# Attention and highway layer in one kernel: query turns in quarters of the array, one shared turning place, a new list of steps

## The chip, the cores and the metric

The kernel runs on one core of one Trainium2 chip. The metric is the device time of one execution in microseconds (us), lower is better. Five engines work side by side, each through its own instructions in order: TensorE (PE, matrix products and turns), VectorE (DVE), ScalarE (ACT), GpSimd (POOL) and SyncE (SP, which here only issues DMA transfers). TensorE writes to PSUM, eight banks of 2 KiB for each of the 128 partitions. Semaphores make one engine wait for another.

## The reference

Linear attention over 8 batches of 8 heads, 576 rows and 64 columns a head, then a highway layer over the 4608 rows of 512 columns that the heads give together:

```python
q_s = softmax(q, axis=-1)                    # over the 64 columns of a head
k_s = softmax(k, axis=2)                     # over the 576 rows
kv  = einsum('bhsd,bhse->bhde', k_s, v)
x   = einsum('bhsd,bhde->bhse', q_s, kv)     # -> rows b*s, columns h*d
H   = maximum(x @ w_h, 0)
T   = 1 / (1 + exp(-(x @ w_t + b_t)))
out = T * H + (1 - T) * x
```

All inputs and the output are float32; 30.4 MB are read and 9.4 MB written.

## The kernel before, in words

The rows are worked in 36 tiles of 128. A batch gives four tiles, and each pair of batches a ninth that takes the last 64 rows' worth of both (tiles 0 to 3 batch 0, 4 to 7 batch 1, 8 both, 9 to 12 batch 2, and so on; lines 125 to 129). Tiles 0, 4 and 5 are worked in two halves.

For a batch b the steps are, by their names in the list:

- `k`, `q`, `v`, `w`, `b`: transfers in, all on SP but the bias.
- `eq`, `ek` (ACT): exponentials of the queries and keys to float16; `vc` (POOL, some on ACT or DVE): v to float16.
- `kv` (PE): for each pair of heads 64x64 products of 65 columns (the 65th sums the keys), 72 a batch, on the four quarters of the array in turn (L269). `kr`, `kn` (DVE): the quotient, written into a block form for two heads at once.
- `qt` (PE): turns of the exponentials of the queries, so that the head's columns lie on the partitions; three groups a batch, of 8, 8 and 2 turns of 128x128 (L319, L324). They go into PSUM tile `qps`, which has a bank of its own. `qc` (DVE or ACT, L333) copies them to `eq` in SBUF. Two groups of batch 7 are turned by DMA instead (`qd`).

For a tile i:

- `xu` (PE, L361): turned queries times kv, with the sums in a 65th column; `rs`, `x` (DVE, L370 and L376): the quotient, to x in float16.
- `xt` (PE, L384): four turns of x into PSUM tile `turned`; `xe` (DVE or ACT, L391) copies them to `xT`.
- `bw`: the bias into the bank `tps`, as an ACT copy of a broadcast bias (L399) or as a PE product with ones (L401). `mt` (PE, L411): four products of x with w_t on top. `mh` (PE, L419): four products with w_h / 2 (less the identity, `whd` and `whc` at the start), into `gps`.
- `th` (ACT): tanh of half of it; `dd` (DVE, L439): the relu part; `uu`: (1 + tanh) times that, in one DVE instruction (L453) or in two on POOL (L450, L451; `:P` in the list); `oo` (POOL, L471): plus x; `st`: the store.

The order is written out by hand: `ORDER` (lines 16 to 62) is a list of 683 steps, each with the engine after a colon where there is a choice, and the kernel emits them in that order under a manual schedule. Each engine's instructions stand in the list's order, and a step waits for the steps ahead of it in the list that touch what it touches. `fill` steps are products of zeros into `turned` that keep PE at work at the start. PSUM: `tps` two banks, `gps` two, `xu` and kv two together, `qps` one, `turned` one.

The start of the list runs: loads of batch 0, w_h, w_t, then batch 1 (`k_1_2 v_1_2 q_1_0 k_1_0 v_1_0 q_1_4`). The loads of k, q and v have three buffers each, so that a load waits for the batch three back.

Of the kernel before, what the change touches and what calls it, by code (L numbers as in the profile page):

```python
# [8 lines left out]
FP32 = mybir.dt.float32  # L9
# [12 lines left out]
wtc_2:P whc_2:A mh_1_0 wtc_0:P vc_1_3 ek_1_3 ek_1_2 vc_1_0 xe_3_0:D mh_3_0 dd_1 xt_0_1 xt_0_0 mt_1_0 xe_0_0:D mh_0_0
xe_0_1 dd_3 xt_2_0 mh_0_1 mt_0_1 th_1_0 xe_2_0:D dd_0 vc_1_2:A kv_1_1 uu_1_0 oo_1_0 eq_1_0 mt_0_0 th_0_0 ek_1_0 ek_1_1
kr_1_1 bw_3 qt_1_0 vc_1_1:A kn_1_1 qc_1_0 mt_3_0 xu_5_1 uu_0_0 mh_2_0 th_3_0 bw_2 rs_5_1 x_5_1 dd_2 xu_4_1 kv_1_0
kr_1_0 eq_1_1 rs_4_1 xt_5_1 mt_2_0 th_2_0 kn_1_0 bw_5 xe_5_1:D x_4_1 xu_5_0 mt_5_1 qt_1_1 eq_1_2 rs_5_0 x_5_0 xt_5_0
xu_4_0 bw_4:A uu_3_0:P oo_3_0 xe_5_0:D mh_5_1 rs_4_0 x_4_0 mh_5_0 xt_4_1 qc_1_1:A xt_4_0 xe_4_1:D dd_5 eq_2_0 xe_4_0:D
v_4_0 mt_5_0 th_5_0 xu_6_0 qt_1_2 rs_6_0 qc_1_2 oo_0_0 mt_4_1 mh_4_1 mh_4_0 uu_2_0:P x_6_0 mt_4_0 eq_2_1 xt_6_0 xu_8_0
uu_5_0 bw_6:A xe_6_0:D qt_2_0 rs_8_0 x_8_0 mh_6_0 oo_5_0 th_4_0 xt_8_0 dd_4 uu_4_0 xu_7_0 mt_6_0 ek_2_0:F rs_7_0
vc_2_2:A bw_8 xe_8_0:D mt_8_0 x_7_0 th_6_0 xt_7_0 th_8_0 oo_2_0 vc_2_0 kv_2_0 oo_4_0 qc_2_0 q_4_0 bw_7:A qt_2_1
qc_2_1:A dd_6 uu_6_0:P oo_6_0 eq_3_0:F xe_7_0:D kr_2_0 kn_2_0 mh_8_0 xu_9_0 rs_9_0 x_9_0 mt_7_0 th_7_0 bw_9 dd_8  # L30
uu_8_0:P qt_2_2 qc_2_2:A xu_10_0 bw_10:A xt_9_0 xe_9_0:D rs_10_0 x_10_0 ek_3_0 mh_7_0 dd_7 ek_3_2 mh_9_0 xu_12_0 k_4_0
xt_10_0 k_5_0 rs_12_0 qt_3_0 xe_10_0:D x_12_0 mt_9_0 th_9_0 uu_7_0:P q_4_9 dd_9 xu_11_0 qc_3_0 vc_3_2:A xt_12_0
mt_10_0 rs_11_0 mh_10_0 x_11_0 v_5_0 q_5_0 vc_3_0 st_1_1 q_5_9 uu_9_0 dd_10 oo_7_0 kv_3_0 qt_3_1 th_10_0 oo_8_0 st_1_0
xe_12_0 bw_12:A mh_12_0 kr_3_0 qc_3_1:A kn_3_0 xu_14_0 rs_14_0 x_14_0 bw_11:A xt_11_0 xe_11_0 mt_12_0 th_12_0 qt_3_2
v_6_0 xt_14_0 oo_9_0 k_6_0 xu_13_0 q_6_0 xe_14_0 mh_11_0 dd_12 qc_3_2 mt_11_0 rs_13_0 eq_4_0:F th_11_0 uu_12_0
uu_10_0:P x_13_0 dd_11 xu_15_0 rs_15_0 vc_4_0 mh_14_0 x_15_0 st_5_1 dd_14 qt_4_0 oo_10_0 vc_4_2 xu_16_0 rs_16_0 x_16_0
# [24 lines left out]
st_35_1:A
"""


@with_exitstack
def kernel(
    ctx: ExitStack,
    tc: tile.TileContext,
    q: bass.AP,
    k: bass.AP,  # L70
    v: bass.AP,
# [5 lines left out]
    nc = tc.nc  # L77
# [456 lines left out]
```

## Time and profile before

| what | value |
|---|---|
| median of 3 runs | 119.03 us (119.0 to 119.74) |
| span of the profiled execution, first to last instruction | 116.9 us |
| lies around the span, against the median | 2.1 us |
| instructions | 3424 |
| HBM read, written | 30.41 MB, 9.44 MB |
| granted TensorE clock, mean | 0.995 |

The profiled execution's own time outside its span isn't in the profile; the median stands for it. In rows of groups the columns are line, engine, operation, output and inputs with shapes, count, then busy us and mean ns of one, then idle us ahead of them and what ended it. In the timeline and in the chain the first two numbers are the start and the length in us. A length of a PE row holds the pipeline's latency: the next step starts before that length is over. Busy times by stretch have busy us and counts of PE, PEld (weight load), DVE, ACT and POOL, then granted clock, DMA share and GB/s.

### The profile page before, as it was taken

The numbers are of one execution on the slowest core, as the hardware profiler recorded it, in microseconds if no ns is written. First come the engines' busy times: TensorE is split into PE (matmuls) and PEld (weight loads), VectorE is DVE, ScalarE is ACT, GpSimd is POOL, SyncE is SP. The second block draws the span as 40 slices with busy tenths as digits, with TensorE's granted clock in tenths as the row PEclk, the third lists the DMA queues.
The fourth block names the chain that finished last, engine by engine and source line by source line (L and its number), as shares of the span: only waits on it lengthen the run. The fifth ranks groups of instructions, "written<-read, shape, count | busy, mean of one in ns | idle before, by whom it ended". The sixth has DMA issues, their size and how long they took to land.

```text
span 116.9 us, 3424 instructions
## 1 busy us (share of the span) xinstructions
PE 109.5 (94%) x1351; PEld 61.6 (53%) x1351; DVE 93.3 (80%) x222; ACT 90.0 (77%) x132; POOL 89.1 (76%) x99
## 2 busy tenths in 40 slices
PE   5999987999999999999999999999999999999930
PEld 2354544545665656565665547566564555554520
DVE  5642587589799979979889798988989887899870
ACT  4356461897999999989999999998597998545520
POOL 5022237208996999999999999999989699999960
PEclk9999999999999999999999999999999999999998
DMA  2999999999999999999999999999999956992875
GB/s 42 399 392 377 408 398 385 375 377 379 393 391 397 383 391 393 358 375 387 357 376 360 387 392 363 390 381 383 399 398 217 302 204 270 397 404 115 315 295 179
DMA packets 24195, 40.58 MB, mean 347 GB/s; under 512 B 5362, under 2 KB 11762, under 8 KB 24180
## 3 DMA queue, kind: packets, MB, share of 16 engines
q1 hardware_dynamic: 24032, 40.24, 96.9%
q8 instruction: 10, 0.16, 0.6%
q10 hardware_dynamic: 148, 0.14, 0.4%
q14 instruction: 5, 0.04, 0.1%
HBM read 30.41 MB, written 9.44 MB: 341 GB/s over the span
## 4 chain that ended last, share of the span: by engine, by line
PE 67%; POOL 15%; issue 6%; DVE 5%; DMA 3%; SPq 1%; POOLq 0%; DVEq 0%
PE tps L411 18%; PE gps L419 16%; PE turned L167 9%; POOL o L471 7%; PE xu L361 6%; PE turned L384 5%; PE kv L269 5%; PE qps L324 4%; POOL u L451 4%; DMA out_dram<-o 3%; POOL g L450 2%; PE qps L319 2%; POOL v L259 2%; DVE x L376 2%; PE tps L401 1%
## 5 line engine op out<-in xcount | busy, mean ns | idle before, releaser
L471 POOL TENSOR_TENSOR o<-u,x 128x512 f32<-128x512 f16 (+1 forms) x36 | 40.6, 1143 | 1.6 <-DVE u L453 0.7
L411 PE MATMUL tps<-w16t,xT 128*128 128x512 f16 (+1 forms) x148 | 37.3, 373 | 0.0
L419 PE MATMUL gps<-w16h,xT 128*128 128x512 f16 x144 | 36.8, 379 | 0.5 <-DVE xT L391 0.5
L376 DVE TENSOR_TENSOR x<-xu,rs 128x512 f16<-128x512 f32 (+1 forms) x39 | 25.2, 649 | 2.4
L259 POOL CAST v<-v 128x1152 f16<-128x1152 f32 (+1 forms) x14 | 14.0, 1010 | 14.7 <-DMA v<-in_v_dram 13.7
L439 DVE SCALAR_TENSOR_TENSOR d<-x,gps 128x512 f16<-128x512 f16 x36 | 24.5, 680 | 0.3
L451 POOL TENSOR_TENSOR u<-g,d 128x512 f16<-128x512 f16 x17 | 19.7, 1158 | 1.7 <-DVE rs L370 0.4
L253 ACT ACTIVATE ek<-k 128x576 f16<-128x576 f32 (+2 forms) x15 | 17.9, 1225 | 3.0 <-DMA k<-in_k_dram 3.0
L419 PEld LDWEIGHTS <-xT 128*128 128x128 f16 x144 | 13.0, 98 | 12.3 <-DVE xT L391 1.8
L399 ACT COPY tps<-ball 128x512 f32<-128x512 f32 x28 | 16.6, 597 | 3.5 <-DVE u L453 3.2
L411 PEld LDWEIGHTS <-xT 128*128 128x128 f16 x148 | 13.2, 98 | 10.6 <-DVE xT L391 0.4
L361 PE MATMUL xu<-kvb,eq 128*128 128x130 f16 (+1 forms) x160 | 14.8, 224 | 0.2 <-DVE kvb L287 0.2
L384 PE MATMUL turned<-idh,x 128*128 128x128 f16 x144 | 14.2, 220 | 0.5 <-DVE x L376 0.5
L391 DVE COPY xT<-turned 128x512 f16<-128x512 f16 (+1 forms) x28 | 10.9, 391 | 4.2 <-PE turned L384 3.0
L435 ACT ACTIVATE tps<-tps 128x512 f32<-128x512 f32 (+1 forms) x20 | 11.2, 559 | 3.6 <-PE tps L411 3.3
L453 DVE SCALAR_TENSOR_TENSOR u<-tps,d 128x512 f16<-128x512 f32 (+1 forms) x19 | 12.7, 671 | 1.4 <-ACT tps L435 0.6
L361 PEld LDWEIGHTS <-eq 128*128 128x128 f16 (+1 forms) x160 | 10.0, 100 | 7.3 <-DVE x L376 2.5
L167 PE MATMUL turned<-blank 128*128 128x512 f16 x40 | 12.4, 458 | 1.5 <-POOL blank L149 1.3
L384 PEld LDWEIGHTS <-x 128*128 128x128 f16 x144 | 9.8, 98 | 6.0 <-DVE x L376 2.1
L307 ACT ACTIVATE qe<-q 128x1024 f16<-128x1024 f32 (+3 forms) x9 | 9.4, 1052 | 4.1 <-DMA q<-in_q_dram 4.1
L450 POOL TENSOR_SCALAR g<-th 128x512 f16<-128x512 f16 x17 | 10.6, 621 | 0.9 <-ACT th L433 0.9
L433 ACT ACTIVATE th<-tps 128x512 f16<-128x512 f32 x17 | 10.0, 594 | 0.9 <-PE tps L411 0.9
(48 smaller groups left out, 106.8 us busy)
## 6 DMA issues: line engine op xcount, KB each, us to landing
k<-in_k_dram SPq DMA_DIRECT2D x6, 1152.0 KB, 12.2
v<-in_v_dram SPq DMA_DIRECT2D x6, 1152.0 KB, 12.0
out_dram<-o SPq DMA_DIRECT2D x23, 256.0 KB, 4.0
q<-in_q_dram SPq DMA_DIRECT2D x10, 512.0 KB, 11.5
out_dram<-o SPq DMA_DIRECT2D x6, 512.0 KB, 3.8
k<-in_k_dram SPq DMA_DIRECT2D x4, 576.0 KB, 9.3
q<-in_q_dram SPq DMA_DIRECT2D x2, 1152.0 KB, 14.2
q<-in_q_dram SPq DMA_DIRECT2D x2, 640.0 KB, 10.5
```

What stands on the lines that cost most here:

```text
L167: nc.tensor.matmul(spare, blank[:, 0:P], blank, start=True, stop=True, skip_group_check=True)
L253: nc.scalar.activation(t[:, :, c:c + n].rearrange("p j c d -> p c j d"), T[f"k32{b}"][:, c:c + n].rearrange("p c (j d) -> p c j d", j=NJ), ...
L259: copy(v16[b % NV][:, c:c + n, :, 0:D], T[f"v32{b}"][:, c:c + n].rearrange("p c (j d) -> p c j d", j=NJ))
L361: nc.tensor.matmul(dst, turned_q(b, jp, n), kvb[b % NKV][:, hh, kk], start=True, stop=True, skip_group_check=True)
L376: nc.vector.tensor_mul(t[:, k0:k1], sums(i, k)[:, :, :, 0:64], T[f"rs{i}_{k}"][:, 0:k1 - k0].unsqueeze(3).to_broadcast([P, k1 - k0, 4, D]))
L384: nc.tensor.matmul(t[:, n], T[f"x{i}"][:, n0 + n % 2:n0 + 2 * P:2], idh, is_transpose=True, start=True, stop=True, skip_group_check=True)
L399: nc.scalar.copy(t[:, cs], ball[:, cs])
L411: nc.tensor.matmul(T[gate(i, k)][:, cs], T[f"xT{i}"][:, n], w16["t"][:, n, cs], start=False, stop=(n == parts[-1] and not first), skip_gro ...
L419: nc.tensor.matmul(t, T[f"xT{i}"][:, n], w16["h"][:, n], start=(first and n == parts[0]), stop=(n == parts[-1] and not (first and len(part ...
L439: nc.vector.scalar_tensor_tensor(t, T[f"x{i}"], -0.5, T[f"gps{i}"], op0=ALU.mult, op1=ALU.max)
L451: nc.gpsimd.tensor_mul(t, g, T[f"d{i}"])
L471: eng.tensor_add(t[:, cs], T[f"u{i}_{h}"][:, cs], T[f"x{i}"][:, cs])
```

## The change

- `qps` and its bank are gone. `turned` is now one PSUM tile of two banks, for turns of queries and of x alike. Query turns of the old kind lie in bank 0; x turns lie in bank 1, even tiles in its first half, odd tiles in its second.
- Query turns of batches 2 to 6, groups 0 and 1 (ten groups), are done by 32 turns of 64x64 on the four quarters of the array, the two halves of the rows into the two banks, so that such a group takes half of both banks. `qc` reads it from there in one instruction.
- `bw` can be a DVE copy (`:D`): 11 are, 19 are on ACT (28 before) and 7 on PE (9 before).
- The list is new (680 steps): w_t is loaded ahead of w_h, and batch 1 comes as `k_1_2 v_1_2 q_1_0 q_1_4 k_1_0 v_1_0`; 26 fill products where there were 40; 21 tiles have `uu` on POOL (17 before); 21 `xe` steps on DVE and 18 on ACT (28 and 11); 12 casts of v on POOL and 7 on ACT, five of these of the large kind (14 and 5, two large); one cast of w_t on ACT.

```diff
-    ps_q = pool("ps_q", 1, space=PS)
-    ps_xt = pool("ps_xt", 1, space=PS)
+    ps_ab = pool("ps_ab", 1, space=PS)
...
-    turned = ps_xt.tile([P, 2, 4, P], FP16, tag="xtps", name="turned")
-    spare = turned.rearrange("p a c d -> p (a c d)").bitcast(FP32)
+    turned = ps_ab.tile([P, 2, 2 * DM], FP16, tag="ab", name="turned")
+    spare = turned[:, 1].bitcast(FP32)
...
+    QUADS = (2, 3, 4, 5, 6)
+
+    def corners(b, g):
+        return b in QUADS and g < 2
+
+    def qt_corners(b, g):
+        t = turned[:, :, g * DM:(g + 1) * DM]
+        for n in range(8):
+            for r in range(2):
+                rows = slice(64 * r, 64 * r + 64)
+                for c in range(2):
+                    cols = slice(64 * c, 64 * c + 64)
+                    if b in WIDE:
...
+                        src = main[rows, 2 * g + n // 4, n % 2, n % 4 // 2, cols]
+                        dst = t[cols, r, 64 * n:64 * n + 64]
+                    else:
+                        j, kk = n // 2, n % 2
+                        src = T[f"qe{b}"][rows, 4 * g + j, 2 * kk + c]
+                        dst = t[cols, r].rearrange("p (a k t s u) -> p a k s t u", a=2, k=2, s=2, u=2)[:, j % 2, kk, j // 2]
+                    nc.tensor.matmul(dst, src, idh[rows, rows], is_transpose=True, start=True, stop=True,
+                                     skip_group_check=True)
+
     def qt(e, b, g):
+        if corners(b, g):
+            qt_corners(b, g)
+            return
         j0, j1 = GROUPS[g]
         a, s = (2, 2) if g < 2 else (1, 1)
-        t = T[f"qps{b}_{g}"] = ps_q.tile([P, a, 4, s * NP], FP16, tag="qps", name=f"qps_{b}_{g}")
+        t = T[f"qps{b}_{g}"] = turned[:, 0, 0:a * 4 * s * NP].rearrange("p (a n t) -> p a n t", a=a, n=4)
...
+        if corners(b, g):
+            src = turned[:, :, g * DM:(g + 1) * DM]
+            if b in WIDE:
+                copy(t.rearrange("p a n (r t) -> p r (a n) t", r=2), src.rearrange("p r (m t) -> p r m t", m=8))
+            else:
+                copy(t.rearrange("p a (k r) t -> p r (a k) t", r=2), src.rearrange("p r (m t) -> p r m t", m=4))
+            T[f"eq{b}_{g}"] = t
+            return
...
     def xt(e, i, k):
         k0, k1 = heads(i, k)
-        t = T[f"xtps{i}"] = turned[:, 0]
+        t = T[f"xtps{i}"] = turned[:, 1, i % 2 * DM:(i % 2 + 1) * DM].rearrange("p (n t) -> p n t", n=4)
...
     def bw(e, i, h=0):
-        bank = (ps_t, "tps") if i < LAST or h == 0 else (ps_q, "qps")
-        t = T[gate(i, h)] = bank[0].tile([P, DM], FP32, tag=bank[1], name=f"tps_{i}_{h}")
+        if i < LAST or h == 0:
+            t = T[gate(i, h)] = ps_t.tile([P, DM], FP32, tag="tps", name=f"tps_{i}_{h}")
+        else:
+            t = T[gate(i, h)] = turned[:, 0].bitcast(FP32)
...
+        elif e == "D":
+            nc.vector.tensor_copy(t[:, cs], ball[:, cs])
```

Stretches of the new list that matter below. The opening, from the weights on:

```
+b_0 q_0_0 v_0_1 setupdve k_0_0 b_32 eq_0_0 bsplit setuppool fill_5 fill_8 bp ek_0_0 fill_6 v_0_0 v_0_2 vc_0_2 ek_0_1
...
+fill_4 vc_0_0 vc_0_1:D k_0_2 ek_0_3 v_0_3 vc_0_3 kv_0_0 kr_0_0 qt_0_0 qc_0_0 q_0_4 ek_0_2 kv_0_1 w_t_2 w_t_0 wtc_0:P
+kn_0_0 xu_0_0 kr_0_1 kn_0_1 xu_1_0 xu_0_1 bw_2 rs_1_0 rs_0_0 x_0_0 w_h_0 whd_0:P x_1_0 whd_1:P w_h_2 whd_2:P eq_0_1
+qt_0_1 k_1_2 wtc_2 v_1_2 q_1_0 xt_0_0 rs_0_1 x_0_1 xt_1_0 xe_1_0:D xe_0_0:D xt_0_1 xe_0_1:D bc whd_3:P vc_1_3 bw_1:A
+mt_1_0 qc_0_1:A th_1_0 whc_0:A fill_3 xu_2_0 bw_0:D mt_0_0 mh_0_0 whc_2:A mt_0_1 th_0_0 bw_6:A rs_2_0 q_1_4 k_1_0
+ek_1_3 ek_1_2 x_2_0 xt_2_0 xu_3_0 mh_1_0 rs_3_0 xe_2_0:D x_3_0 vc_1_2:A mh_0_1 dd_0 xt_3_0 mt_2_0 eq_1_0 th_2_0 mh_2_0
+dd_1 uu_1_0:P v_1_0 kv_1_1 dd_2 qt_1_0 kr_1_1 qc_1_0 xe_3_0 mh_3_0 eq_1_1 kn_1_1 eq_1_2 ek_1_0 ek_1_1 vc_1_0:A
+uu_0_0:P qt_1_1 qc_1_1 oo_0_0 vc_1_1 eq_0_2 q_2_0 xu_4_1 bw_3 mt_3_0 rs_4_1 x_4_1 xu_5_1 rs_5_1 uu_2_0:P th_3_0 dd_3
+uu_3_0:P oo_3_0 kv_1_0 kr_1_0 kn_1_0 bw_4 xt_4_1 xe_4_1 k_2_0 xu_4_0 qt_0_2 qc_0_2:A xu_6_0 x_5_1 mh_4_1 rs_4_0 x_4_0
```

Batches 4 and 5, and tiles 25 and 26:

```
+mt_15_0 uu_10_0:P xe_14_0 dd_13 kv_4_0 qt_4_1 uu_13_0 th_15_0 bw_14:A oo_10_0 eq_5_0 kr_4_0 kn_4_0 oo_13_0 qc_4_1:A
+qt_4_0 qc_4_0 mh_15_0 xu_17_0 rs_17_0 dd_15 x_17_0 mh_14_0 dd_14 xt_16_0 xe_16_0 mt_14_0 xu_18_0 rs_18_0 mh_16_0
+bw_16:A xt_17_0 q_5_9 x_18_0 th_14_0 uu_14_0 eq_5_1 xe_17_0 oo_11_0 vc_5_0 xu_21_0 bw_17:A rs_21_0 xt_18_0 uu_15_0:P
...
+dd_22 xe_26_0:D k_7_0 rs_29_0 xt_25_0 xe_25_0 mt_24_0 q_6_9 x_29_0 th_24_0 mt_26_0 bw_25:D xu_27_0 mh_26_0 v_7_0
```

More of the change, by code (lines that the diff above doesn't have):

```diff
@@ L22 @@
[L22 to L36, printed above, removed]
@@ new lines @@
+xe_7_0:D qc_2_0 vc_2_0:A mh_6_0 x_8_0 bw_7:D mh_7_0 xt_5_1 xt_8_0 xe_8_0 xe_5_1:D xt_5_0 xe_5_0:D mt_7_0 qt_2_1
+qc_2_1:A th_7_0 bw_5:D dd_7 k_3_0 vc_2_2 kv_2_0 mh_8_0 mt_5_1 dd_6 eq_3_0:F kr_2_0 kn_2_0 bw_8:D xu_9_0 rs_9_0 x_9_0
+mh_5_1 mh_5_0 dd_5 mt_5_0 xu_12_0 oo_2_0 v_3_0 uu_6_0:P rs_12_0 th_5_0 xt_9_0 uu_7_0:P xe_9_0:D x_12_0 mt_8_0 ek_3_0
+th_8_0 mh_9_0 uu_5_0 xt_12_0 oo_7_0 dd_8 xu_10_0 k_4_0 xe_12_0 rs_10_0 x_10_0 bw_9 mt_9_0 oo_6_0 oo_5_0 ek_3_2 xt_10_0
+uu_8_0 xu_11_0 xe_10_0:D mh_12_0 rs_11_0 x_11_0 dd_9 qt_3_0 dd_12 vc_3_0:A v_4_0 bw_10:A qt_3_1 vc_3_2 th_9_0 kv_3_0
@@ new lines @@
+xt_20_0 q_6_0 dd_21 oo_17_0 st_14_0 bw_18:A xu_23_0 rs_23_0 x_23_0 xe_20_0:D qt_5_1 qt_4_2 st_14_1 mt_18_0 vc_6_0:A
+xu_22_0 th_19_0 qc_5_1 st_5_1 rs_22_0 st_12_1 vc_6_2 qc_4_2 mh_19_0 bw_20:A x_22_0 xt_23_0 xe_23_0:D th_18_0 dd_19
+q_7_0 dd_18 uu_21_0:P st_12_0 mt_20_0 eq_6_1 eq_6_0 kv_6_0 uu_19_0:P kr_6_0 th_20_0 kn_6_0 qt_6_0 qt_6_1 oo_19_0
+uu_18_0 oo_18_0 qc_6_0:A st_7_0 mh_23_0 xu_24_0 rs_24_0 qt_5_2 xt_22_0 bw_23:A mh_20_0 xe_22_0 bw_22:A x_24_0 xu_25_0
+xt_24_0 oo_21_0 xe_24_0 mt_23_0 eq_7_1 th_23_0 mt_22_0 qc_5_2 th_22_0 dd_23 rs_25_0 x_25_0 xu_26_0 dd_20 uu_20_0:P
@@ new lines @@
+bw_28:A qd_7_0 rs_28_0 oo_24_0 x_28_0 mh_27_0 xu_31_0 st_1_1 eq_6_2 bw_27:A dd_30 xt_28_0 uu_25_0:P xe_28_0 dd_27
+rs_31_0 mt_27_0 mt_28_0 oo_29_0 x_31_0 th_27_0 q_7_9 uu_27_0 xu_33_0 xt_31_0 xe_31_0:D mh_28_0 st_21_0 qt_6_2 oo_25_0
+st_16_1 mh_31_0 uu_30_0:P rs_33_0 x_33_0 oo_30_0 th_28_0 dd_28 dd_31 bw_31:A xt_33_0 st_10_0 xe_33_0 eq_7_2 oo_27_0
+st_25_0 xu_32_0 rs_32_0 x_32_0 mt_31_0 bw_33:D qc_6_2:A th_31_0 uu_31_0 oo_31_0 mh_33_0 xt_32_0 xe_32_0:D xu_34_0
+rs_34_0 qt_7_2 st_30_0 st_26_0 x_34_0 qc_7_2:A uu_28_0:P mt_33_0 th_33_0 dd_33 mh_32_0 xt_34_0 bw_32:A uu_33_0 oo_33_0
@@ L62 @@
+oo_28_0 xe_34_0 xu_35_0 rs_35_0 st_23_0 x_35_0 bw_34:A st_5_0 st_31_0 mt_32_0 th_32_0 mh_34_0 st_33_0 dd_32 uu_32_0
+st_10_1 st_28_0 xt_35_0 oo_32_0 mt_34_0 xe_35_0 dd_34 mh_35_0 bw_35_0 bw_35_1 th_34_0 uu_34_0 oo_34_0 st_32_0 dd_35
+st_34_0 mt_35_0 th_35_0 mt_35_1 th_35_1 uu_35_0 oo_35_0 st_35_0 uu_35_1 oo_35_1:D st_35_1:A
 """
```

45 lines of the change are left out of this document (15 added, 30 removed).

## The prediction

> **What bounds the kernel now.** I read first the page, then the busy times by stretch, then the chain of waits inside the long middle stretch, then the groups and the opening of the timeline.
>
> ```profile
> span 116.9 us, 3424 instructions
> ```
>
> ```profile
> 0.00:20.00 20.00, 17.39 (x164) 8.39 (x165) 11.85 (x40) 9.65 (x13) 6.74 (x17) 1.00 0.94 342
> 20.00:39.00 19.00, 19.00 (x230) 10.30 (x231) 15.73 (x42) 17.11 (x24) 11.91 (x14) 1.00 1.06 384
> 39.00:93.00 54.00, 53.98 (x797) 32.22 (x792) 48.21 (x106) 50.15 (x70) 51.56 (x52) 1.00 1.08 369
> 93.00:117.00 24.00, 19.09 (x206) 10.68 (x193) 17.53 (x37) 13.05 (x27) 18.89 (x19) 0.98 0.71 271
> ```
>
> The columns are PE, PEld, DVE, ACT, POOL, clock, DMA share, GB/s. From 39 to 93 us nothing is loose: of 54.0 us POOL works 51.6, ACT 50.2, DVE 48.2, and PE never seems to stop. A busy PE is not PE at its peak, so its real pace is taken from the chain:
>
> ```profile
> 58.14 0.88 PE tps L411 x4
> 59.02 0.76 PE kv L269 x72
> 60.33 0.86 PE gps L419 x4
> 62.28 0.23 PE xu L361 x4
> 62.51 0.22 PE turned L384 x4
> 70.69 0.45 PE qps L319 x8
> ```
>
> One tile costs PE 0.86 (w_t) + 0.86 (w_h) + 0.23 (xu) + 0.22 (turn of x) = 2.17 us; a query turn of eight 0.45; a batch of kv 0.76. Put against the list of steps, the PE steps from batch 2's kv (39 us) to batch 7's (93 us) sum to 52.2 us: PE is 97% packed there, with 1.8 us loose, and it leads the chain. After 93 us PE has 18.8 us of work in 24 and the end hangs on POOL, whose last two o end at 113.4:
>
> ```profile
> 111.61 1.82 POOL L471 TENSOR_TENSOR o<-u,x 128x512 f32<-128x512 f16 x2 [0.49 <-DVE u L453]
> ```
>
> **The change, part by part.** The durations:
>
> ```profile
> L471 POOL TENSOR_TENSOR o<-u,x 128x512 f32<-128x512 f16 x35 | 40.0, 1157 | 1.6 <-DVE u L453 0.7
> L451 POOL TENSOR_TENSOR u<-g,d 128x512 f16<-128x512 f16 x17 | 19.7, 1158 | 1.7 <-DVE rs L370 0.4
> L450 POOL TENSOR_SCALAR g<-th 128x512 f16<-128x512 f16 x17 | 10.6, 621 | 0.9 <-ACT th L433 0.9
> L259 POOL CAST v<-v 128x1152 f16<-128x1152 f32 x10 | 11.3, 1147 | 1.0 <-PE tps L411 0.9
> L376 DVE TENSOR_TENSOR x<-xu,rs 128x512 f16<-128x512 f32 x33 | 22.8, 690 | 2.2
> L399 ACT COPY tps<-ball 128x512 f32<-128x512 f32 x28 | 16.6, 597 | 3.5 <-DVE u L453 3.2
> L433 ACT ACTIVATE th<-tps 128x512 f16<-128x512 f32 x17 | 10.0, 594 | 0.9 <-PE tps L411 0.9
> L302 ACT ACTIVATE qe<-q 128x1024 f16<-128x1024 f32 x6 | 6.4, 1061 | 0.0
> L333 ACT COPY eq<-qps 128x1024 f16<-128x1024 f16 x6 | 6.1, 1009 | 0.4 <-PE qps L324 0.3
> L391 DVE COPY xT<-turned 128x512 f16<-128x512 f16 x23 | 9.5, 413 | 2.7 <-PE turned L384 1.5 <-ACT tps L435 0.7
> L391 ACT COPY xT<-turned 128x512 f16<-128x512 f16 x10 | 5.9, 589 | 2.1 <-PE turned L384 2.1
> ```
>
> *Quarter turns.* Ten groups (batches 2 to 6, two each) go from 8 turns of 128x128 to 32 of 64x64. The trace has no 64x64 turn, but kv is a 64x64 product of 65 columns in the same order of quarters, and there are half-array products:
>
> ```profile
> 57.38 0.42 PE L361 MATMUL xu<-kvb,eq 128*64 128x130 f16 x8
> 57.74 0.40 PE L384 MATMUL turned<-idh,x 128*128 128x128 f16 x4
> 57.98 1.03 PE L411 MATMUL tps<-w16t,xT 128*128 128x512 f16 x4
> 59.00 0.77 PE L269 MATMUL kv<-v,ek 64*64 64x65 f16 x72
> 59.71 0.62 PE L319 MATMUL qps<-idh,qe 128*128 128x128 f16 x8
> 60.16 1.03 PE L419 MATMUL gps<-w16h,xT 128*128 128x512 f16 x4
> 61.03 0.39 PE L384 MATMUL turned<-idh,x 128*128 128x128 f16 x4
> ```
>
> 72 kv products start within 0.71 us (59.00 to 59.71): 9.9 ns each, so 32 take 0.32 and a group saves 0.13, 1.3 us in all. But kv started only when the product ahead of it had ended (57.98 + 1.03 = 59.01), while a 128x128 step starts 0.16 us before that end (60.16 + 1.03 = 61.19 against 61.03). Entering quarters costs 0.16. The new list puts eight of the ten groups beside a kv or beside each other; two entries are new: 0.3. I take -1.0 us. Bounds: half of 0.45 each, -2.3 with no entries; above, the pace of the 128x64 row (8 in 0.36 us, 45 ns each), 32 in 1.44, +10 us. The kv row is nearest, the shape being the same.
>
> The Trainium skill, page TensorEngine Tiling (Array Packing), section Key Properties, says that a change of tiling mode drains the array; the 0.16 us agrees. Without grouping, by that rule, ten entries would cost 1.6 us and the quarters would save nothing.
>
> *One turning place for all.* Before, query turns have a bank of their own and x turns another. Now all lie in one tile of two banks. In the changed program as built, every turn waits for the copies out of that tile that stand ahead of it in the list, whichever half they read: the turn of tile 25 (odd half) waits for the copy of tile 26 (even half), the second query turn of batch 4 for the copy of the first, tile 32's turn for the copy of query turn 6_2; copies on ACT and DVE wait for each other too. So the second place for x buys no overlap. What is forced is at least the copy, less the PE work that stands between. In the old list no pair is short (least work 0.56 us, against 0.41 for a DVE copy). In the new one, after 39 us:
> - batch 4, second query turn: between w_t of tile 15 and that turn PE holds only kv_4 and the first turn, 0.76 + 0.32 = 1.08 us. ACT must by then do, in its order, tanh 15 (0.59), bias 14 (0.60), exponentials of batch 5 (1.06) and the copy (1.01): 3.26 us, the tanh not before the w_t product ends. PE idle 2.2 us at least; behind it stand w_h of tile 15, xu 17 and all else.
> - tile 25 straight after 26 (DVE): 0.4.
> - tile 18 after 17 with one xu between (ACT): 0.59 - 0.23 = 0.4.
> - query turn 5_1 after tile 20 with one xu between (DVE): 0.41 - 0.23 = 0.2.
>
> Together 3.2 us. PE's 1.8 loose us cover part and +1.4 is left, which I take; bounds 0 (other engines were late anyway) and +3.2. Tile 5's second half after tile 8 (an ACT copy and half a DVE one) falls before 39 us, where ACT rather than PE is late, and query turn 7_2 in the tail, where PE has slack: nothing for both.
>
> The Trainium skill, page PSUM — Partial Sum Buffer, section PSUM bank collisions raise a hardware error, asks that engines be kept apart by bank, not by address. By that rule the waits between the two halves of x stay and only those between the banks (turns 6_2, 7_2) are avoidable: by it the sum stays; by addresses alone tiles 18 and 25 would wait for nothing and it would be 0.8 us less. No run here shows two engines in one bank.
>
> *w_t ahead of w_h, and batch 1's queries ahead of its keys.*
>
> ```profile
> 13.86 0.88 POOL L226 TENSOR_TENSOR w32h<-w32h,idf 128x128 f32<-128x128 f32 x2 [2.44 <-DMA w32h<-in_moe_w_h_dram]
> 19.01 1.04 POOL L222 CAST w16t<-w32t 128x1024 f16<-128x1024 f32 x1 [0.27 <-DMA w32t<-in_moe_w_t_dram]
> 22.03 0.67 POOL L259 CAST v<-v 128x576 f16<-128x576 f32 x1 [1.98 <-DMA v<-in_v_dram]
> 26.56 0.67 POOL L259 CAST v<-v 128x576 f16<-128x576 f32 x1 [3.86 <-DMA v<-in_v_dram]
> 27.19 1.16 POOL L471 TENSOR_TENSOR o<-u,x 128x512 f32<-128x512 f16 x1
> ```
>
> ```profile
> 16.97 1.06 ACT L232 ACTIVATE w16h<-w32h 128x1024 f16<-128x1024 f32 x1
> 22.41 0.65 ACT L259 CAST v<-v 128x576 f16<-128x576 f32 x1
> 23.46 1.06 ACT L307 ACTIVATE qe<-q 128x1024 f16<-128x1024 f32 x1 [0.40 <-DMA q<-in_q_dram]
> 24.98 1.26 ACT L253 ACTIVATE ek<-k 128x576 f16<-128x576 f32 x2
> ```
>
> ```profile
> 27.47 0.48 PE L269 MATMUL kv<-v,ek 64*64 64x65 f16 x36
> ```
>
> The last weight lands at 19.0 in both. Now it is w_h, and still needs 0.88 (POOL) and 1.06 (ACT): whole at 21.0. From there ACT's list up to v of batch 1's first half is two tanh 1.2, bias 0.6, four key pieces 2.5, two v casts 1.3, two query pieces 2.1, the last ninth of the queries about 0.4 (an estimate, between a quarter of 1.06 and a half), one x copy 0.6: 8.7 us, to 29.7. (That v lands 655 KB later: 26.5 + 0.655/0.384 = 28.2, so ACT, not DMA, decides.) Batch 1's second kv starts at 29.7, before at 27.5. Counted through both lists, PE then has 80.7 us of work left (old prices); before, at that moment, 79.6. The w_t products come earlier but run into this: +1.3 with rounding. Bounds: -1.0 if nothing is late (PE packed from 21.0 on), +2.
>
> *Bias copies.* PE loses two products (in the counts above), ACT nine copies (-5.4 us), DVE gains eleven. DVE's price is not in the trace: between 0.41 (L391) and 0.69 (L376); I take 0.62, near the latter, which moves f32 too: 6.8 us, against four u fewer (2.7) and seven x copies fewer (2.9). DVE +1.2, ACT +1.3 net (seven x copies 4.1, five large v casts where two were, a w_t cast). POOL +3.3: four more u at 1.78, less three large and one more small cast, less a w_t cast. DVE and ACT stay below PE in the middle: nothing added. Queues: v_7 is now the last big load; with 32.9 MB up to its end (loads, ten store halves) and 6.8 + 7.3 MB moved by 39 us (342 and 384 GB/s), it lands by 39 + 18.8/0.369 = 90 us. POOL's cast of it has 21.6 us of POOL work behind it and so comes at about 92; k_7 lands earlier: nothing. Transposes and stores follow the loads on SP, as now.
>
> **Sum.** +1.3 - 1.0 + 1.4 = +1.7 us on PE's path: span 118.6. The median of the runs shown, 119.03, lies 2.1 above the profiled span; with the same around it, 120.7.
>
> **The rivals.**
> - *POOL decides and starts earlier: faster.* POOL's packed run starts at 27.2 now. In the new list its first tiles' u come sooner: tile 1's g follows v at 22.7. Work from there is 36 o (41.2), 21 g and u (37.4) and 8 casts (8.7), 87.3 us, against 82.8 from 27.2. Without gaps it ends at 110.0, 3.4 us before the 113.4 of now; I count 2.8, since the last tile's chain waits for DVE (0.49) either way. It decides if PE's forced waits hide behind POOL's queue. Against it: w_t first gives POOL no d before w_h is there. Time 119.0 - 2.8 = 116.2.
> - *The waits are absorbed.* PE's 1.8 us loose and slack on ACT take the 3.2: +1.3 - 1.0 = +0.3, 119.3.
> - *Quarter turns are slow*, 45 ns each: +10 us, 129. The kv row speaks against.
>
> **How the numbers follow.** Forecast (slower, about 120.7) 0.47; absorbed 0.18; faster 0.32; slow quarters 0.03. About 1% is what a measurement can tell from no change. Slower by over 1%: 0.50, within: 0.18, faster: 0.32. Low end: the rival's 116.2, a little lower for its bounds, 115.8. High end: start +2, all of the 3.2 and no gain from quarters (entries eat it): +5, 124.0. The likeliest case's own range is 120.2 to 123.
>
> **What would show it.** Right: PE idle of about 2 us after batch 4's kv, ended by the ACT copy of query turn 4_1; short ones at tiles 18 and 25; batch 1's second kv near 29.7 us; 32 quarter turns in about 0.3 us. Wrong: no such gaps, POOL over 97% busy from 23 us on and an earlier end, or turns of a group spread over 1 us.

## The result, and the profile after

The changed kernel takes 138.58 us (median, 137.17 to 139.0) against 119.02 for the kernel before on the same chip: ratio 1.1615, 95% interval 1.155 to 1.1681. The forecast was 120.7 us, its range 115.8 to 124.0: the sign is right, the size is not. In some of the kernels below the granted clock differed from run to run; their ratios go by the runs near their fastest.

The head of the page after (busy us and share, TensorE's row of 40 slices, its clock):

```profile
span 136.4 us, 3891 instructions
...
PE 110.4 (81%) x1575; PEld 61.2 (45%) x1575; DVE 94.7 (69%) x223; ACT 93.0 (68%) x132; POOL 92.2 (68%) x104
...
PE   6975779688968999968398896945977989998960
...
PEclk9998699999999999999999999998699999999998
```

Every engine is busy for nearly the same time as before; what has grown is the time for which each of them stands. Busy time by stretch of the kernel after, cut at the starts of kv of batches 2, 4, 5, 6 and 7 (columns as in the prediction):

```profile
0.00:20.00 20.00, 14.90 (x142) 7.94 (x143) 9.94 (x38) 10.46 (x14) 6.33 (x17) 0.91 0.93 342
20.00:42.60 22.60, 18.86 (x270) 10.08 (x270) 15.33 (x40) 17.63 (x27) 17.39 (x19) 1.00 1.06 385
42.60:64.70 22.10, 20.36 (x355) 11.35 (x342) 19.09 (x42) 19.50 (x23) 18.90 (x20) 1.00 1.07 370
64.70:79.40 14.70, 11.49 (x213) 6.43 (x216) 10.02 (x22) 10.48 (x16) 11.45 (x12) 1.00 0.90 323
79.40:89.20 9.80, 8.37 (x188) 4.86 (x190) 7.82 (x19) 7.87 (x10) 5.55 (x6) 1.00 0.89 281
89.20:112.00 22.80, 17.26 (x247) 9.85 (x248) 14.54 (x31) 14.98 (x22) 14.90 (x15) 0.93 0.68 227
112.00:136.40 24.40, 19.16 (x203) 10.67 (x202) 17.96 (x37) 12.08 (x25) 17.67 (x18) 0.98 0.45 173
```

The length of a stretch less TensorE's busy time (the number behind the comma) is TensorE's idle time: 5.1, 3.7, 1.7, 3.2, 1.4, 5.5, 5.2, together 26.0 us. Before it was 7.4, all of it in the first 20 us (2.6) and in the tail (4.8). So 18.6 of the 19.5 us that the span has grown by are idle time of TensorE, nearly all of it between 0 and 112 us; the other 0.9 is longer busy time (stretches at a lower clock add to it, quarter turns take from it). What TensorE waited for, the longest rows of its waits in the kernel after (us in total, times, longest):

```profile
PE turned L329 <- issue: 3.5, 1, 3.5
PE turned L417 <- DVE xT L424: 2.8, 3, 1.4
PE turned L329 <- ACT eq L361: 2.3, 1, 2.3
PE xu L394 <- DVE x L409: 2.2, 3, 1.2
PE xu L394 <- DVE kvb L285: 1.7, 3, 0.7
```

The third row is the wait that the prediction named (batch 4's second query turn, forecast 2.2). Of the others its sum held only 0.69 us of the second (the turn of tile 25, forecast 0.4). Two of them show what was missing. The fourth, at 60.4 us, in three timelines of the kernel after, ScalarE, VectorE, TensorE:

```profile
56.87 2.16 ACT L251 ACTIVATE ek<-k 128x2304 f16<-128x2304 f32 x1
58.90 0.40 ACT L366 COPY eq<-turned 128x256 f16<-128x256 f16 x1
```

```profile
59.32 0.43 DVE L424 COPY xT<-turned 128x512 f16<-128x512 f16 x1 [1.36 <-ACT eq L366]
59.66 0.68 DVE L409 TENSOR_TENSOR x<-xu,rs 128x512 f16<-128x512 f32 x1
```

```profile
60.40 0.41 PE L394 MATMUL xu<-kvb,eq 128*128 128x130 f16 x4 [1.16 <-DVE x L409]
```

A small query copy stands on ScalarE behind 2.16 us of exponentials; VectorE's copy of x, from the same tile, has to wait for it, x behind that is late, and with it TensorE. No turn is part of this wait. The first row is of another kind (timeline of TensorE, kernel after):

```profile
89.15 0.78 PE L267 MATMUL kv<-v,ek 64*64 64x65 f16 x72
89.75 0.55 PE L329 MATMUL turned<-idh,qe 64*64 64x64 f16 x42
93.79 0.38 PE L329 MATMUL turned<-idh,qe 64*64 64x64 f16 x22 [3.49 <-issue]
94.09 1.48 PE L456 MATMUL gps<-w16h,xT 128*128 128x512 f16 x4
```

TensorE stops in the middle of batch 6's quarter turns, with no engine to wait for, and the product behind takes 1.48 us instead of 1.03: the clock row has its dip there.

### The profile page after: what moved, and what is told of

Its sections match the earlier page's. It is cut to its first block, busy times and chain, and to the rows that moved or that the text cites. A ratio compares the mean times of both kernels' runs of the same rounds, so it can differ in the third digit from the quotient of the medians.

```text
span 136.4 us, 3891 instructions
## 1 busy us (share of the span) xinstructions
PE 110.4 (81%) x1575; PEld 61.2 (45%) x1575; DVE 94.7 (69%) x223; ACT 93.0 (68%) x132; POOL 92.2 (68%) x104
## 4 chain that ended last, share of the span: by engine, by line
PE 46%; DVE 18%; ACT 16%; issue 7%; DMA 5%; POOL 4%; SPq 2%; DVEq 0%; ACTq 0%; POOLq 0%
PE gps L456 15%; PE tps L448 13%; PE turned L417 5%; DMA k<-in_k_dram 5%; PE xu L394 4%; ACT ek L251 4%; DVE x L409 4%; PE kv L267 3%; DVE d L476 3%; ACT xT L424 3%; PE turned L329 3%; POOL o L508 3%; DVE xT L424 2%; DVE tps L436 2%; ACT th L470 2%
## 5 line engine op out<-in xcount | busy, mean ns | idle before, releaser
L456 PE MATMUL gps<-w16h,xT 128*128 128x512 f16 x144 | 37.9, 389 | 1.5 <-ACT xT L424 1.4
L488 POOL TENSOR_TENSOR u<-g,d 128x512 f16<-128x512 f16 x21 | 24.3, 1155 | 15.9 <-DVE rs L403 7.1
L424 ACT COPY xT<-turned 128x512 f16<-128x512 f16 (+1 forms) x18 | 10.1, 564 | 12.1 <-PE turned L417 9.9
L257 POOL CAST v<-v 128x1152 f16<-128x1152 f32 (+1 forms) x12 | 11.3, 945 | 9.3 <-DMA v<-in_v_dram 9.3
L470 ACT ACTIVATE th<-tps 128x512 f16<-128x512 f32 x21 | 12.4, 597 | 2.8 <-PE tps L448 2.8
L487 POOL TENSOR_SCALAR g<-th 128x512 f16<-128x512 f16 x21 | 13.0, 617 | 1.8 <-ACT th L470 1.1
L403 DVE RECIPROCAL rs<-xu 128x8 f32<-128x8 f32 (+1 forms) x39 | 7.5, 196 | 8.5 <-PE xu L394 8.3
L424 DVE COPY xT<-turned 128x512 f16<-128x512 f16 (+1 forms) x21 | 8.2, 395 | 6.3 <-PE turned L417 3.6
L472 ACT ACTIVATE tps<-tps 128x512 f32<-128x512 f32 (+1 forms) x15 | 8.6, 572 | 5.4 <-PE tps L448 5.4
L490 DVE SCALAR_TENSOR_TENSOR u<-tps,d 128x512 f16<-128x512 f32 (+1 forms) x15 | 10.0, 668 | 2.4 <-ACT tps L472 1.3
```

What stands on the lines that cost most here:

```text
L424: copy(t[:, 2 * k0:2 * k1], T[f"xtps{i}"][:, 2 * k0:2 * k1])
L456: nc.tensor.matmul(t, T[f"xT{i}"][:, n], w16["h"][:, n], start=(first and n == parts[0]), stop=(n == parts[-1] and not (first and len(part ...
L470: nc.scalar.activation(T[f"th{i}"], src, AF.Tanh, scale=0.5)
L487: nc.gpsimd.tensor_scalar(g, T[f"th{i}"], 1.0, 1.0, op0=ALU.add, op1=ALU.mult)
L488: nc.gpsimd.tensor_mul(t, g, T[f"d{i}"])
```

## The experiments

Theories. A: the one tile makes copies and turns wait for each other. B: the new list itself costs, whatever the tiles. C: short instructions run faster than they are supplied. All ratios are to the kernel before, with 95% intervals; times are medians in us.

### List and tile apart

list_alone: the new list over the tiles before. Four query turns (3_1, 2_2, 4_2, 6_1) stand behind the copies ahead of them, as in new_list_shared below.

```diff
-    ps_ab = pool("ps_ab", 1, space=PS)
+    ps_q = pool("ps_q", 1, space=PS)
+    ps_xt = pool("ps_xt", 1, space=PS)
-        t = T[f"xtps{i}"] = turned[:, 1, i % 2 * DM:(i % 2 + 1) * DM].rearrange("p (n t) -> p n t", n=4)
+        t = T[f"xtps{i}"] = turned[:, i % 2]
```

> The changed kernel's list of steps (with its bias copies and its opening) over the PSUM tiles of the kernel before: a bank for the query turns by 128 rows, another for the turns of x, five steps shifted so that no query turn overwrites one not yet copied. Theory A (the one tile for both kinds of turn makes copies on ScalarE and VectorE and turns on TensorE wait for each other): without it the time falls back to 119 to 123 us. Theory B (the new list itself: its later start of batch 1, its stores ahead of loads, its bunched steps): it stays at 131 to 138 us. Theory C (the 64-row turns of batch 6 run faster than their instructions arrive, 3.5 us of TensorE standing, and a lower clock after it): there are no such turns here, 131 to 135 us, with no stand of issue behind kv of batch 6.

old_list: the program after, the list before. In it the second group of batch 6's quarter turns falls on the turn of tile 25 that isn't copied yet, so that part of the output isn't the reference's.

> The list of steps of the kernel before, with the program of the changed one: the one tile for both kinds of turn and the turns in quarters for batches 2 to 6. Theory A (the one tile): 126 us or more, since the old list was not laid out for it. Theory B (the list): 118 to 121 us. Theory C (instruction supply): in the old list the turns of batch 6 do not follow its kv directly, so no stand; 118 to 121 us, and another figure only if a stand of issue is seen elsewhere.

old_list_shared: the same without quarters.

```diff
-    QUADS = (2, 3, 4, 5, 6)
+    QUADS = ()
```

> The list of steps of the kernel before and the one tile for both kinds of turn, but no turns in quarters. Theory A (the one tile): within 2 us of the same kernel with quarters, so 126 us or more. Theory B (the list): 119 to 122 us. Theory C (the quarters): 119 to 121 us, and where the kernel with quarters is slower than this one, the difference is theirs.

new_list_shared: that edit in the changed kernel, with its own list (qt_3_1, qt_2_2, qt_4_2, qt_6_1 behind the copies ahead of them).

> The changed kernel (new list, one tile for both kinds of turn) without turns in quarters: all query turns by 128 rows in the first bank, five steps shifted so that none overwrites one not yet copied. So far: old list and own tiles 118.8 us, old list and one tile 134.3, new list and own tiles 131.4, new list with one tile and quarters 138.6. If the costs of list and tile added up, 146 us. Supply theory: the 3.49 us stand and the low clock behind it go, 132 to 135 us, kv of batch 6 to kv of batch 7 some 17.5 us instead of 22.8. Theory A in its strong form (the waits on the one tile make the whole difference between 131.4 and 138.6): 137 to 139 us.

| list | tiles | quarters | kernel | us | ratio |
|---|---|---|---|---|---|
| old | own | no | before | 119 | 1 |
| old | one | no | old_list_shared | 134.28 | 1.1303 (1.1274 to 1.1333) |
| old | one | yes | old_list | 134.0 | 1.1269 (1.1233 to 1.1306) |
| new | own | no | list_alone | 131.39 | 1.105 (1.1013 to 1.1087) |
| new | one | no | new_list_shared | 135.18 | 1.1365 (1.1293 to 1.1436) |
| new | one | yes | after | 138.58 | 1.1615 (1.155 to 1.1681) |

A and B are both true, and they don't add: the tile alone costs 15 us in the old list and 4 in the new one, the list alone 12. The quarters are worth nothing in the old list and cost 3 us in the new one. The waits agree for the tile in the new list: TensorE's waits for x, 2.2 us in the kernel after, are 1.4 in new_list_shared and 0.3 in list_alone.

Where the tile costs, in old_list_shared (timelines of TensorE and VectorE):

```profile
65.32 0.61 PE L344 MATMUL turned<-idh,qe 128*128 128x128 f16 x8
...
69.38 0.38 PE L417 MATMUL turned<-idh,x 128*128 128x128 f16 x4 [1.70 <-DVE eq L366]
```

```profile
65.59 0.69 DVE L476 SCALAR_TENSOR_TENSOR d<-x,gps 128x512 f16<-128x512 f16 x1
66.20 0.21 DVE L403 RECIPROCAL rs<-xu 128x8 f32<-128x8 f32 x1
66.51 0.69 DVE L409 TENSOR_TENSOR x<-xu,rs 128x512 f16<-128x512 f32 x1
67.12 0.41 DVE L424 COPY xT<-turned 128x512 f16<-128x512 f16 x1
67.73 0.21 DVE L403 RECIPROCAL rs<-xu 128x8 f32<-128x8 f32 x1 [0.19 <-PE xu L394]
68.04 0.69 DVE L409 TENSOR_TENSOR x<-xu,rs 128x512 f16<-128x512 f32 x1
68.65 0.68 DVE L366 COPY eq<-turned 128x1024 f16<-128x1024 f16 x1
```

The query turn is done at 65.93 and copied at 69.33, 3.4 us later, because six instructions stand ahead of the copy on VectorE. With a bank of its own no turn of x has to wait for that copy; now the next one does.

### The stand with issue

turns_apart: in the changed kernel one step moved.

```diff
-kn_6_0 qt_6_0 qt_6_1 oo_19_0
+kn_6_0 qt_6_0 oo_19_0
...
-mh_20_0 xe_22_0
+mh_20_0 qt_6_1 xe_22_0
```

> The changed kernel with one step moved: the second group of 32 quarter turns of batch 6 stands some ten steps later, behind a matmul with w_h, so that 208 small instructions follow each other instead of 272. Theory C (supply): the stand of 3.49 us falls below 1 us and the clock holds; with what hangs on it 131 to 135 us. Theories A and B: 137 to 139 us, no change that can be measured.

138.5 us, ratio 1.1669 (1.159 to 1.1747): no gain in time, where theory C asked for 131 to 135, though the stand was shorter in its profile. The starts of kv show where the time went. From batch 6's kv to batch 7's it takes 19.6 us (91.88 to 111.44), the kernel after 22.8 (89.15 to 111.97), new_list_shared 17.5 (90.30 to 107.83). But batch 6's kv starts 2.7 us later than in the kernel after: in this profile the clock is 0.50 for 10.2 us in the opening, with the same list there, against 3.4, and for 3.4 us more at 70 us. The mean clock of its four runs is 0.938 to 0.947, that of the kernel after 0.944 to 0.972. So the shorter stand is worth some 3 us where it lies; why the clock is lower ahead of it isn't settled.

Timeline of TensorE in turns_apart, and then in after_spaced (below), which has the same move:

```profile
91.88 0.78 PE L267 MATMUL kv<-v,ek 64*64 64x65 f16 x72
92.48 0.44 PE L329 MATMUL turned<-idh,qe 64*64 64x64 f16 x32
92.86 1.04 PE L456 MATMUL gps<-w16h,xT 128*128 128x512 f16 x4
93.86 0.41 PE L394 MATMUL xu<-kvb,eq 128*128 128x130 f16 x4
94.11 0.27 PE L349 MATMUL turned<-idh,qe 128*128 128x128 f16 x2
95.44 0.38 PE L417 MATMUL turned<-idh,x 128*128 128x128 f16 x4 [1.06 <-issue]
```

```profile
87.00 0.27 PE L349 MATMUL turned<-idh,qe 128*128 128x128 f16 x2
90.74 0.38 PE L417 MATMUL turned<-idh,x 128*128 128x128 f16 x4 [3.46 <-issue]
```

Count from kv's first product to the stop: 72 + 42 = 114 in the kernel after, 72 + 32 + 4 + 4 + 2 = 114 in these two. It stops at the same instruction number, whatever stands there: not a wait for data. The page after counts what the instruction queue of DMA moved, and a narrow stretch of its DMA (91 to 92.5 us) holds one of these transfers, while 89 to 91 holds none:

```profile
q8 instruction: 12, 0.20, 0.6%
```

```profile
q8 instruction: 1, 0.02, 4.3%
```

The 12 transfers are 0.20 MB together, that is 16 KB each (10 before, 0.16 MB). The 320 quarter turns, in the place of 80 turns, are 480 instructions more with their weight loads, for two transfers more: about 240 instructions in each. A block comes between the stop at 90.3 us and the restart at 93.8; in after_spaced one lies between 88 and 89.5, inside its stand from 87.3 to 90.7. So at the end of a block TensorE waits for the next.

The traces of the other kernels settle it. There are seven stands with issue in all of them together, in six kernels. Counted from the start over everything that a trace lists for TensorE (products, weight loads and a few others), they lie behind instruction 2497 in the kernel after, turns_apart, after_spaced and after_old_bias (below), behind 1729 in after_spaced too (0.73 us), behind 2241 in tiny_behind_kv6 (next) and behind 961 in old_list (0.89 us): always whole multiples of 256 apart. Each time TensorE goes on 1.3 to 1.6 us after the end of a block's transfer (92.27 to 93.79 in the kernel after). Ahead of these stands 256 instructions ran in 3.1 to 5.0 us; where a block took 5.3 us or more, no kernel has such a stand, and in the kernel before it takes 7.2 us at least.

The Trainium skill, page Runtime: NRT & Kernel Launch, section Instruction fetch mechanics, has blocks of 16 KiB or 256 instructions, which agrees, and calls the crossing mostly hidden; here one costs up to 3.49 us.

tiny_behind_kv6 and tiny_apart: the kernel before with 64 turns of zeros more.

```diff
-xe_19_0:D kv_6_0
+xe_19_0:D kv_6_0 tiny_16
```

```diff
-mt_21_0
+mt_21_0 tiny_8
...
-mt_24_0
+mt_24_0 tiny_8
```

> The kernel before, with 64 extra turns of 64 by 64 (of zeros, to places that nobody reads) right behind kv of batch 6, so that 272 short instructions follow each other as in the changed kernel. Supply theory: TensorE stands with issue for 2 to 4 us within or behind them, 121.5 to 125 us. If the stand of the changed kernel came from its data or its tile: only their own 0.6 us, 119.2 to 120 us and no stand.

> The same 64 extra turns in the kernel before in two groups of 32, each behind a matmul with w_t and away from kv: 64 short instructions in a row. Supply theory: no stand, 119.2 to 120.5 us, at least 1.5 us under the kernel with all of them behind kv of batch 6. Rival (it is their number or form that costs, not their density): the same time as that kernel.

120.83 us, ratio 1.0162 (1.0128 to 1.0197), and 120.04, ratio 1.0093 (1.0061 to 1.0126). Timeline of TensorE in tiny_behind_kv6:

```profile
82.84 1.04 PE L430 MATMUL gps<-w16h,xT 128*128 128x512 f16 x4 [1.06 <-issue]
```

It lies 4 us behind the last extra turn, at the end of the block that holds them all. Density gives a stand in a kernel that had none, and apart there is none: C holds, though the stand is 1.06 us instead of the 2 to 4 expected, and the two kernels differ by 0.8 us instead of 1.5 at least. How long a stand is depends on when the block comes: in turns_apart its transfer begins 1.4 us ahead of the stop (92.94 and 94.38), in after_spaced 0.8 behind it (88.12 and 87.28), after the same instructions from batch 6's kv on, and they stand for 1.06 and 3.46. What sets the beginning of a transfer isn't settled.

### The opening and the clock

new_opening: the kernel before, its list up to kn_1_0 replaced by the new one's, with its engines for casts and bias copies (bw_6 left at its old place); tiles as in list_alone.

> The kernel before with the new list's opening up to the normalised kv of batch 1 (w_t ahead of w_h, another order of the first five tiles, fewer fills), then the old list's steps as far as not yet done. My forecast of this part was 1.3 us: 120.3 us. Opening theory (gaps of TensorE and a clock halved for 3 to 9 us, nothing after it to catch up, since TensorE was busy to 99% behind 20 us): 122 to 124 us. Rival (the lag is made good): 119 to 119.7 us.

warm_opening: that, with 11 fill products more.

```diff
-vc_0_3 kv_0_0 kr_0_0 qt_0_0 qc_0_0
+vc_0_3 fill_4 kv_0_0 kr_0_0 qt_0_0 qc_0_0 fill_2
...
-kv_0_1
+kv_0_1 fill_3
...
-xu_0_0
+xu_0_0 fill_2
```

> The kernel before with the new opening (123.0 us), and eleven more matmuls of zeros in the places where TensorE stood for 0.4 to 1.4 us, so that it is busy throughout as in the old opening. Clock theory: the granted clock stays at 1.00 (it was 0.50 from 12 to 22 us) and the time is 120.5 to 121.5 us. Order theory (the gaps and the later first tiles cost, the clock does not): 122.5 us or more.

list_old_opening: the other way round, list_alone with the old list up to kn_1_0.

> The new list over the old tiles (131.4 us), with the old list's opening up to the normalised kv of batch 1, its order of w_h and w_t and its fills; then the new list's steps as far as not yet done. Opening theory: in the new opening TensorE has gaps of 0.4 to 0.9 us and the granted clock falls to half from 13 us on; with the old one it stays at 1.00, kv of batch 2 starts 3 to 4 us earlier, 127 to 128.5 us. Waits theory (what counts is the turns that stand right behind copies not yet made, later in the list): time gained in the opening is lost at the next waits, 130 to 131.5 us.

123.01 us, ratio 1.0334 (1.0299 to 1.0369); 120.82, 1.0156 (1.0131 to 1.0182); 131.2, 1.1002 (1.0925 to 1.108). TensorE's busy time and clock (second number and third from the end) in new_opening, then in warm_opening:

```profile
8.00:10.00 2.00, 0.70 (x4) 0.20 (x2) 0.00 (x0) 0.47 (x1) 1.25 (x2) 1.00 1.06 392
10.00:12.00 2.00, 1.49 (x66) 1.19 (x68) 0.86 (x2) 1.26 (x2) 0.69 (x2) 0.87 1.09 375
12.00:14.00 2.00, 0.86 (x37) 0.55 (x26) 1.33 (x5) 1.06 (x1) 0.00 (x0) 0.50 1.02 400
```

```profile
8.00:10.00 2.00, 2.00 (x11) 0.93 (x10) 0.00 (x0) 0.28 (x1) 1.27 (x2) 1.00 1.05 388
10.00:12.00 2.00, 2.00 (x65) 1.11 (x67) 0.64 (x2) 1.26 (x2) 0.67 (x1) 1.00 1.10 381
12.00:14.00 2.00, 1.88 (x46) 0.87 (x38) 1.55 (x6) 1.18 (x2) 0.00 (x0) 1.00 1.01 402
```

Products of zeros bring 2.2 of the 4.1 us back: half of the opening's price is the clock, halved after 4 us (8 to 12) in which TensorE worked 2.2. The old list's fills did that job. But in the new list the old opening gains nothing that can be measured (1.1002 against 1.105): batch 1's second kv starts 3.6 us earlier than in list_alone (27.50 against 31.10), batch 2's only 1.3 (41.79 against 43.08), batch 5's no longer (79.63 against 79.36). What was saved is lost at the next waits and, between batches 4 and 5, in 3.4 us at half clock behind a wait of 2.2.

### The bias copies

bias_three: the kernel before, 14 bias copies on the engines of the new list (11 on VectorE, 1 on ScalarE, 2 on TensorE). list_old_bias, spaced_old_bias and after_old_bias: the reverse (14 copies, in spaced_old_bias 12), in list_alone, list_spaced (below) and the changed kernel.

```diff
-bw_11:A bw_12:A bw_15:A bw_21:A bw_24:A bw_25:A bw_33:A bw_7:A bw_0 bw_5 bw_8 bw_4:A bw_13:A bw_1
+bw_11:D bw_12:D bw_15:D bw_21:D bw_24:D bw_25:D bw_33:D bw_7:D bw_0:D bw_5:D bw_8:D bw_4 bw_13 bw_1:A
```

> The kernel before with the changed kernel's choice of engine for each bias copy: eleven on VectorE (0.69 us each in the changed kernel's trace), one on ScalarE, two back on TensorE. My forecast of this part was nothing: 118.7 to 119.5 us. Rival (VectorE, busy 17.4 of 20 us, is late with x and its copies, and TensorE waits): 120 to 122 us.

> The new list over the old tiles (131.4 us), each bias copy back on the engine that it had before. Sum theory (the bias copies' 6.6 us and the opening's 4.1 us act in the new list as they did in the old one): 124 to 126 us. Rival (the waits of the new list's order come last anyway, and VectorE is not late there, since TensorE's waits are on ScalarE's copies): 129.5 us or more.

> The new list with the old opening and the moved turns (126.1 us), each bias copy back on its old engine. Sum theory: what is left over the kernel before, 7.2 us, is nearly all the bias copies' 6.6: 119 to 121 us. Rival (the order still holds waits of its own on ScalarE, which gets eleven copies of 0.6 us back): 123 us or more.

> The whole changed kernel (138.6 us) with the bias copies on the engines that they had before. Sum theory: 6 to 7 us less, 131.5 to 133 us. Rival (in the changed kernel the waits on the one tile and the stand with issue come last, and hide what VectorE loses): 136 us or more.

bias_three 125.53 us, ratio 1.0543 (1.0509 to 1.0577). The reverse costs too: list_old_bias 134.94, 1.1233 (1.1166 to 1.1299) against 1.105; spaced_old_bias 128.55, 1.0819 (1.0764 to 1.0875) against 1.0589. In the changed kernel nothing is shown: after_old_bias 141.89, without an interval, its lowest, 139.19, next to 138.58. The sum theory falls in all three. A copy's group, and one wait in bias_three, VectorE and TensorE:

```profile
L400 DVE COPY tps<-ball 128x512 f32<-128x512 f32 x11 | 7.6, 688 | 1.0 <-ACT ball L246 0.8
```

```profile
77.53 0.68 DVE L332 COPY eq<-qps 128x1024 f16<-128x1024 f16 x1
78.13 0.68 DVE L400 COPY tps<-ball 128x512 f32<-128x512 f32 x1
```

```profile
78.86 1.02 PE L412 MATMUL tps<-w16t,xT 128*128 128x512 f16 x4 [1.02 <-DVE tps L400]
```

The copy comes behind a query copy, and the product with w_t needs it first. Back on ScalarE in the new list, the bias copies make ScalarE late instead (TensorE's waits in spaced_old_bias; the first was 1.6 us in list_spaced, the second is not in it):

```profile
PE turned L383 <- ACT xT L390: 3.1, 5, 1.4
PE tps L412 <- ACT tps L398: 1.2, 1, 1.2
```

### Turns moved away from their copies

after_spaced: the changed kernel with qc_4_1 straight behind qt_4_1, qt_4_0 and qc_4_0 behind xu_17_0, xt_5_0 behind xt_5_1, xe_20_0 behind xt_20_0, xe_17_0 behind th_14_0, xe_3_0 behind xt_3_0, qc_2_2 behind th_12_0, xt_25_0 behind xt_26_0, qt_6_1 behind mh_20_0. list_spaced: the moves that apply, in list_old_opening.

> The changed kernel with eleven steps moved by a few places, nothing else: the copies that TensorE or VectorE waited for are issued earlier (query copy 4_1, pair copy 2_2, the copies of x of tiles 3, 17 and 20), the turns that stood right behind an uncopied one later or together (query turn 4_0, tile 5's second half, tile 25), and the second turn of batch 6 away from its kv. The waits in its trace that this takes away add up to 2.3 + 1.4 + 1.4 + 1.4 + 1.2 + 0.7 + 0.5 = 8.9 us, and 2.4 us of the stand with issue. Waits theory (the order of turns and copies on one tile is what costs): 126 to 130 us. Rival (another resource, such as the loads that the list issues late, sets the pace and takes the place): 134 us or more.

> The new list over the old tiles with the old opening (131.2 us), and the same kind of moves: query copy 4_1 earlier, query turn 4_0 later, pair turn 2_2 later, tile 5's second half next to its first, copies of tiles 17 and 20 earlier, tile 25 behind 26. The waits taken away are 2.2 + 1.1 + 1.5 + 0.7 + 0.5 = 6.0 us and a stretch of halved clock of some 4 us, worth 2. Waits theory: 123 to 126 us. Rival (something else is late next): 128.5 us or more.

after_spaced 131.17 us (127.96 to 133.65), ratio 1.0821 (1.0724 to 1.0918): some 9 us come back by that ratio, about as much as the waits taken away, though its stand with issue was 3.46 us long in the profiled run (132.61 us). list_spaced 126.08, ratio 1.0589 (1.056 to 1.0618): 5 us back, the better part of the 6 + 2, so a little of it met other waits. Neither beats the kernel before, and no run points to a version that does.

## Why the prediction was wrong

- *Quarter turns, -1.0.* The pace was right: 32 take 0.38 us to the next start (37.20 to 37.58), forecast 0.32. A gain of the size forecast is there at first: from batch 2's kv to batch 6's the kernel after takes 46.56 us and new_list_shared 47.58, in one profile of each, with four turns at other places. Over the whole kernel it is gone: old_list and old_list_shared differ by less than their intervals, and in the new list the quarters cost 3 us (1.1615 against 1.1365). The step counted it as good that turns stand beside a kv, since a change of mode costs 0.16. That is what put 136 short products in a row, and from batch 6's kv to batch 7's the kernel after is 5.3 us longer than new_list_shared: a stand of 3.49 us, and 3.4 us at half clock behind it. The supply of instructions, which sets that stand, the step did not consider.
- *One turning place, +1.4.* Its named waits came as forecast: 2.28 us for 2.2 in batch 4, 0.51 for 0.4 at tile 18, 0.69 for 0.4 at tile 25; turn 5_1 1.4 for 0.2, tile 5, counted as nothing, 1.4. The failing step is "What is forced is at least the copy, less the PE work that stands between", used as if it were the whole. "In the old list no pair is short" by that count, and there the tile costs 15 us. A copy ends not its own length after its turn but as late as its engine's list puts it (3.4 us in the example), and copies wait for copies on the other engine. In the new list itself the one tile is worth only 4 us. The 2.2 us in batch 4 is, besides, no price of the one tile: list_alone, with a bank of its own for query turns, has 2.2 there too.
- *"PE's 1.8 loose us cover part".* No run shows that they covered anything. Every stretch of the kernel after has 1.4 us or more of TensorE idle; in new_opening the lag is 3.9 us at batch 2's kv (42.75 against 38.84) and 4.1 at the end.
- *w_t ahead, +1.3.* (The count in it, 80.7 less 79.6, gives 1.1.) In the old list the whole opening costs 4.1 us. Batch 1's second kv starts at 30.66, forecast 29.7, so the order was about right; the clock, half of the price, was not in the sum, although the fills and the clock column were in view.
- *Bias copies, nothing.* 0.69 us each was inside the bounds (0.41 to 0.69). "DVE and ACT stay below PE in the middle: nothing added" is the second failing step: it compares sums of busy time, and what counts is when a copy comes. Alone the new choice costs 6.5 us.
- *Rivals.* POOL over 97% busy and earlier: it is 68% busy. Absorbed: no stretch shows it.

What the parts cost alone, 15, 12, 7, 4 and 3 us, can't be added: the list's 12 already hold the bias copies and the opening, and the tile costs 4 where the list waits anyway. What remains of the new list without its opening, with loosened turns and own tiles is 7 us (list_spaced); which of its other choices (engine of the x copies, of u, of the casts of v, order of stores) makes them is open. So is the gain of two halves of x that wait apart: that needs two engines in one bank, and it wasn't tried.

## What to carry to other kernels

Where four engines, each with its queue in order, are packed to nine tenths, price a change by when each instruction can start on its engine, not by sums of busy time: follow one instruction through the list of its engine up to the one that TensorE waits for. Before two uses share a tile, ask how late each copy out of it may come today without anybody noticing; that slack is the price. Count instructions as well as their time: where 256 of TensorE's ran in 5.0 us or less here, it stood at the end of the block, and a TensorE left half idle for 4 us came back at half clock.

## What the runs showed of the hardware

- TensorE stops at a fixed instruction number until a 16 KB block of its program has come: 3.49 us in the kernel after, 1.06 and 3.46 in two variants, in these three 114 products after the start of batch 6's kv. The places of such a stop in six kernels (961, 1729, 2241, 2497) are multiples of 256 instructions apart, and TensorE goes on 1.3 to 1.6 us after the block's transfer has ended. 256 instructions in 3.1 to 5.0 us came with a stop, in 5.3 us or more without.
- The clock falls to 0.50 without a long stand: single gaps of 0.4 to 1.4 us between 8 and 14 us did it, for 3.4 us in the kernel after and 10.2 in list_alone; with the list of the kernel after up to there, turns_apart has 10.2 too, so the list does not fix the length. The Trainium skill, page TensorE: Matmul & The Clock Gate, section HAM oscillation — how this bites in real kernels, warns of idle gaps over about 3.4 us; none in the opening is that long, so shorter gaps close together are enough. Its section Part 1: The HAM clock gate (the "warmup" mystery) names half and full clock as the two states to be seen, which agrees: the traces here have only 0.50 and 1.00, and what lies between in the rows is a mean.
- A copy of 128x512 f32 from SBUF to PSUM takes VectorE 0.687 us (kernel after) and ScalarE 0.597 (kernel before).
